# One fused kernel of linear attention and two feed-forward layers: the first chunk pipelined by a unit, loads and diagonals moved ahead, two kinds of state products issued together

## The chip, the cores and the metric

The kernel runs on one core of one Trainium2 chip. The metric is device time of one execution in microseconds (us); lower is better. The engines are called PE (matrix products), DVE (vector), ACT (activation), POOL and SP; SP issues the DMAs.

## What is computed

```python
def _attn_ref(r, k, v, w, u):            # B, H, S, D = 4, 8, 768, 48
    for t in range(S):
        cur = np.einsum('bhd,bhe->bhde', u[None] * kt, vt)
        y[:, :, t] = np.einsum('bhd,bhde->bhe', rt, state + cur)
        state = w[None, :, :, None] * state + np.einsum('bhd,bhe->bhde', kt, vt)

def _moe_ref(x, w_in, w_out):            # x: 3072 x 384, d_ff = 2048
    h = x @ w_in
    g = np.where(h > 0.0, h, np.exp(np.minimum(h, 0.0)) - 1.0)
    return g @ w_out

def _moe2_ref(x, w_in, w_out):
    h = x @ w_in
    return (h * np.cos(h)) @ w_out
```

The output is the second layer of the first layer of the attention, all in fp32. A recurrence over 768 steps with a decay per head and channel comes first; its output, as 3072 rows of 384, goes through both layers.

## The kernel before

The sequence is cut into six chunks of 128 steps (`NC`), and the heads into four pairs (`ORDER`, first 3, then 0, 1, 2). A chunk c and a pair j make a unit (c, j), 24 in all; each has the four batches of two heads. Inside a chunk the steps are split once more into an early and a late half of 64. A unit goes through these steps:

- `a_load`: its `trk` (r and k by channel) and `tnat` (r, k and v by time) are loaded. In the first chunk they are called `first_rk` and `first_nat` and lie in buffers of weights that come later.
- `a_scale` (DVE, line 210) multiplies `trk` by powers of the decay. `a_diag` (DVE, lines 224 to 227) forms the diagonal terms `a0`; ACT (line 233) then spreads them over a diagonal matrix `A`, eight instructions. `a_keys` (DVE, line 216 with the table `wn`) scales the keys.
- `gain(c, j, 1)` (PE, line 264) forms the early half's keys-by-values products, `gain(c, j, 0)` the late half's: the state sums. `a_scores` (PE, line 298) forms the scores.
- `a_mask` (DVE) copies the scores into `A` under a mask (line 306) and forms `mid`, the state at the middle of the chunk (line 311).
- `a_out` (PE): the products with `mid` and `st` (line 326), then `values` (line 277) for one half of the scores; `evict` (ACT, line 288) takes the output out of PSUM. `a_state` (DVE, line 337) forms the next state `st`.
- `a_next` does the other `values` of the unit before, the early `gain` and scores of the new one, the eviction and the mask. `a_pack` (SP, line 363) moves the finished output into the rows of `xraw`.

The first chunk runs by itself, unit after unit. While it runs, the first weight is fetched. Then a loop over `t` does the layers: sixteen `t` (tiles f of 128 hidden columns) make a block, one block per chunk and layer. In the first block of the first layer, the weights are unpacked and split as they come: `load_w`, `conv_abs` (ACT, line 86), `conv_low` (DVE, lines 92 and 95), `conv_high` (DVE, lines 102 and 108), `conv_split` (ACT line 131, DVE line 132). `ffn_in` (PE, line 396) makes nine products 128x512 per `t` in groups called wide here; `ffn_out_f32` and `ffn_out_t` (lines 447 and 454) follow two `t` later. `expn` (ACT) and `elu` (DVE, line 414) lie between.

Beside block b, the units of chunk b + 1 are done: `attn_items` sets at which `t` a step of a unit is issued. Each engine runs its instructions in the order in which the program issues them:

```python
            s0 = 4 * n - 3 if c > 1 else 2 + 3 * n
            items.append((s0 - 6, lambda j=j: a_load(c, j)))
            items.append((s0 - 2, lambda j=j: a_scale(c, j)))
            items.append((s0 - 1, lambda j=j: (a_diag(c, j), a_keys(c, j))))
            items.append((s0, lambda j=j, done=done: a_next(done, c, j)))
            items.append((s0 + 1, lambda j=j: (a_out(c, j), a_state(c, j))))
```

`count_safe` checks the decays (PE line 623) for a slower general path, which is not taken with these inputs.

Of the kernel before, what the change touches and what calls it, by code (L numbers as in the profile page):

```python
# [40 lines left out]
def fused_kernel(ctx: ExitStack, tc: tile.TileContext, rk, nat, wcol, urow, r, k, v, wu, w1, w2, out):  # L41
# [178 lines left out]
    def a_diag(c, j):  # L220
        u = units[c, j]
        tnat = u["nat"]
        q, key = (tnat[:, :, i].rearrange("p h e b d -> p h (e b d)") for i in range(2))
        nc.vector.tensor_tensor(out=q, in0=q, in1=key, op=ALU.mult)
        times(tnat[:, :, 0], ub, j)
        a0 = work.tile([P, 2 * B], F32, tag="a0", name="a0")
        nc.vector.tensor_reduce(  # L227
            out=a0.rearrange("p (h n) -> p h n", h=2), in_=tnat[:, :, 0].rearrange("p h e b d -> p h (e b) d"),
            axis=AX.X, op=ALU.add,
        )  # L230
        a = work.tile([P, 2 * B, SC], F32, tag="A", name="A")
        for n in range(2 * B):
            nc.scalar.activation(out=a[:, n], in_=eye, func=AF.Copy, scale=a0[:, n:n + 1])  # L233
        u["A"] = a

    def a_keys(c, j):
        times(units[c, j]["nat"][:, :, 1], wn, j)
# [17 lines left out]
    def gain(c, j, row):  # L255

        tnat = units[c, j]["nat"]
        keys = tnat.rearrange("p h x e b d -> p h (x e b d)")
        rs = slice(64 * row, 64 * row + 64)
# [22 lines left out]
    def evict(c, j, same):  # L282
        u = units[c, j]
        if same:
            u["yu"] = work.tile([RP, 2, 2, 2, SC], F32, tag="yu", name="yu")
        for e in range(2):
            row = e if same else 1 - e
            nc.scalar.activation(out=u["yu"][:, e, :, 1 - row], in_=outs(e)[0:RP, row], func=AF.Copy)

    def a_scores(c, j):  # L290
        trk = units[c, j]["rk"]
        gain(c, j, 1)
        for b in range(B):
            for row in range(2):
                for e in range(2):
                    ks, ts = late_early(row)
                    es = slice(64 * e, 64 * e + D)
                    nc.tensor.matmul(  # L298
                        banks[1 - e][ks, (B + b) * SC:(B + b + 1) * SC], trk[es, b // 2, 1, b % 2, ks],
                        trk[es, b // 2, 0, b % 2, ts], start=True, stop=True,  # L300
                    )
# [11 lines left out]
            op0=ALU.mult, op1=ALU.add,  # L313
        )

    def a_out(c, j):
# [13 lines left out]
        values(c, j, True)  # L330
        if c < NC - 1:
            gain(c, j, 0)
        evict(c, j, True)

    def a_state(c, j):
# [3 lines left out]
                in1=state_sums(0)[0:RP], op0=ALU.mult, op1=ALU.add,  # L339
            )  # L340

    def a_next(done, c, j):

        if done:
            values(*done, False)
        if c < NC:
            a_scores(c, j)
        if done:
            evict(*done, False)
        if c < NC:  # L350
            a_mask(c, j)

    def a_pack(c, j):

# [114 lines left out]
    def general():  # L469

        T, Q = 16, 4
        E = D // Q
        decay = work.tile([P, 2, D], F32, tag="yu", name="decay")
        nc.sync.dma_start(out=decay, in_=wu)
        s = work.tile([P, E, D], F32, tag="nat", name="s", bufs=3)
        nc.vector.memset(s, 0.0)
# [85 lines left out]
                    )  # L562


    def attn_items(c):

        items, packs = [], []
        for n, j in enumerate(ORDER):
            s0 = 4 * n - 3 if c > 1 else 2 + 3 * n
            s1 = 4 * n + 1 if c > 1 or n == HP - 1 else 5 + 3 * n  # L570
            done = (c, ORDER[n - 1]) if n else (c - 1, ORDER[-1]) if c > 1 else None
            items.append((s0 - 6, lambda j=j: a_load(c, j)))
            items.append((s0 - 2, lambda j=j: a_scale(c, j)))
            items.append((s0 - 1, lambda j=j: (a_diag(c, j), a_keys(c, j))))
            items.append((s0, lambda j=j, done=done: a_next(done, c, j)))
            items.append((s0 + 1, lambda j=j: (a_out(c, j), a_state(c, j))))
            if c == NC - 1 and n == HP - 1:
                items.append((s1, lambda j=j: a_next((c, j), NC, None)))
            packs.append((max(s1, 4), lambda j=j: a_pack(c, j)))
        items += packs  # L580
        return items

    def tables():
# [31 lines left out]
    def count_safe():  # L615

        ok = inv
        nc.vector.tensor_scalar(out=ok, in0=wc, scalar1=W_LOW, scalar2=None, op0=ALU.is_ge)
        nc.vector.scalar_tensor_tensor(
            out=ok, in0=wc, scalar=W_HIGH, in1=ok, op0=ALU.is_le, op1=ALU.mult  # L620
        )
        okp = psum.tile([1, HP], F32, tag="h", name="okp", bufs=2)
        nc.tensor.matmul(okp, ones[0:RP], ok, start=True, stop=True)
        nc.vector.tensor_reduce(out=count, in_=okp, axis=AX.X, op=ALU.add)
        nc.vector.tensor_scalar(
            out=safe, in0=count, scalar1=float(RP * HP), scalar2=None, op0=ALU.is_ge
        )

    with tc.manual_schedule():
# [32 lines left out]

        items = {}

        for c in range(NC - 1, 0, -1):
            for it, fn in attn_items(c):
                items.setdefault((c - 1) * NF + it, []).append(fn)
# [4 lines left out]
        table_rows()  # L672
        a_diag(0, ORDER[0])
        a_keys(0, ORDER[0])
        done = None
# [40 lines left out]
        for t in range(NT + 2):  # L716
# [3 lines left out]
            if layer == 0 or t == L:  # L720
                if t < NF - 1:
                    conv_split(t + 1)
                elif block == 1:
                    late_split(f)
                if t > 0:
                    gs[t - 1] = split_g(g) if t > NF else (g,)
                if f == NF - 1 and block + 1 < NC:
                    xs[block + 1] = [split_x(xin[block + 1], k) for k in range(KC)]
                if t == 2 * NF:
                    count_safe()  # L730
                if layer == 0:
# [118 lines left out]
```

## Time and profile before

| | |
|---|---|
| runs | 942.06, 937.43, 942.55 us; median 942.06 |
| profiled execution | 937.57 us, its span 935.9 us |
| PE busy | 893.5 us (95%) |
| DVE busy | 679.4 us (73%) |
| ACT busy | 495.5 us (53%) |
| DMA | 98.90 MB, mean 106 GB/s |
| mean granted clock of PE | 0.993 |

The span is what the trace covers, from the first to the last instruction. Busy shares are means over stages that differ: in the first, there is only the attention of one chunk; in the second, PE and DVE both work on the first block; later PE is busy nearly throughout.

### The profile page before, as it was taken

The page shows a single profiled execution, that of the slowest core. Times are in us where ns is not written, and L with a number is a line of the kernel's source. Part 1 is how long each engine was busy: PE and PEld are TensorE (multiplying, and loading weights), DVE is VectorE, ACT ScalarE, POOL GpSimd, SP SyncE. Part 2 cuts the span into 40 slices and gives each one's busy share as a digit, 9 for nine tenths or more (in the row PEclk, how much of TensorE's full clock was granted, in tenths as well). Part 3 has the DMA queues.
Part 4 walks back from the last instruction along what each step waited for, and adds up shares of the span by engine and source line. Part 5 has one row for each costly group of instructions (what it writes and reads, how often), then busy time and mean ns, then how long its engine had stood idle before and what let it go on. Part 6 is the DMA issues. An engine that isn't in the chain of part 4 may idle for free.

```text
span 935.9 us, 16782 instructions
## 1 busy us (share of the span) xinstructions
PE 893.5 (95%) x6730; PEld 746.4 (80%) x6730; DVE 679.4 (73%) x1164; ACT 495.5 (53%) x998; POOL 4.1 (0%) x18
## 2 busy tenths in 40 slices
PE   5459989999999999999999999999999999999996
PEld 5436556887878888788888899999999999999996
DVE  6579997878776776766534478778777777777775
ACT  2345556666755766656545545445444544444443
POOL 1000000000000000000000000000000000000000
PEclk9979999999999999999999999999999999999999
DMA  9177755444444543441165510200100200200001
GB/s 289 37 216 250 241 160 187 165 139 155 156 134 169 181 159 122 172 148 44 76 221 186 211 57 1 68 1 1 68 1 1 68 0 1 68 1 1 35 1 38
DMA packets 35687, 98.90 MB, mean 106 GB/s; under 512 B 4496, under 2 KB 14352, under 8 KB 35600
## 3 DMA queue, kind: packets, MB, share of 16 engines
q1 hardware_dynamic: 35600, 97.73, 31.3%
q8 instruction: 55, 0.90, 0.4%
q14 instruction: 32, 0.26, 0.1%
HBM read 67.83 MB, written 22.02 MB: 96 GB/s over the span
## 4 chain that ended last, share of the span: by engine, by line
PE 84%; DVE 8%; DMA 2%; ACT 1%; issue 1%; SPq 0%; DVEq 0%
PE ph L396 39%; PE acc L463 21%; PE acc L454 18%; DVE wx L108 1%; PE acc L447 1%; DVE wx L102 1%; PE yb L326 1%; PE yb L264 1%; PE yb L277 1%; PE yb L298 1%; DMA trk<-in_rk 1%; DVE trk L210 1%; DVE wx L95 1%; DVE wx L92 1%; DVE e L414 1%; DMA w<-wx 1%
## 5 line engine op out<-in xcount | busy, mean ns | idle before, releaser
L396 PE MATMUL ph<-xhl,w 128*128 128x512 f32 x1728 | 438.1, 398 | 14.6 <-DVE e L414 9.1
L396 PEld LDWEIGHTS ph<-xhl,w 128*128 128x128 f32 x1728 | 324.8, 189 | 89.0 <-ACT w L131 13.4
L463 PE MATMUL acc<-w,gh 128*128 128x384 f32 x768 | 195.4, 335 | 0.0
L454 PE MATMUL acc<-gh,w 128*128 128x512 f32 x480 | 165.7, 399 | 0.0
L463 PEld LDWEIGHTS acc<-w,gh 128*128 128x128 f32 x768 | 140.0, 188 | 7.9
L439 ACT ACTIVATE r<-r,pair 128x512 f32<-128x512 f32 x96 | 69.5, 724 | 126.7 <-DVE r L433 126.6
L463 PE MATMUL acc<-w,gl 128*128 128x384 f32 x384 | 129.0, 336 | 0.8 <-DVE gl L404 0.8
L427 DVE SCALAR_TENSOR_TENSOR r<-kk,ph 128x512 f32<-128x512 int32 x96 | 66.1, 688 | 62.7 <-ACT kk L422 61.9
L454 PEld LDWEIGHTS acc<-gh,w 128*128 128x128 f32 x480 | 90.1, 188 | 20.6
L414 DVE SCALAR_TENSOR_TENSOR e<-e,ph 128x512 f32<-128x512 f32 x96 | 65.5, 682 | 55.1 <-ACT e L410 55.0
L422 ACT ACTIVATE kk<-ph 128x512 int32<-128x512 f32 x96 | 57.4, 598 | 78.0 <-PE ph L396 78.0
L409 ACT ACTIVATE e<-ph 128x512 f32<-128x512 f32 x96 | 56.9, 593 | 71.3 <-PE ph L396 69.9
L454 PE MATMUL acc<-gl,w 128*128 128x512 f32 x240 | 94.1, 392 | 0.0
L403 ACT ACTIVATE gh<-e 128x512 fp32r<-128x512 f32 x80 | 50.2, 627 | 58.4 <-PE acc L454 54.2
L440 DVE TENSOR_TENSOR r<-r,ph 128x512 f32<-128x512 f32 x96 | 65.8, 686 | 20.9 <-ACT r L439 20.9
L404 DVE TENSOR_TENSOR gl<-e,gh 128x512 fp32r<-128x512 f32 x80 | 55.2, 690 | 33.4 <-ACT gh L403 33.3
L463 PEld LDWEIGHTS acc<-w,gl 128*128 128x128 f32 x384 | 72.1, 188 | 1.4 <-DVE gl L404 1.4
L430 DVE SCALAR_TENSOR_TENSOR r<-kk,r 128x512 f32<-128x512 int32 x96 | 66.4, 692 | 3.3
L404 DVE TENSOR_TENSOR gl<-r,gh 128x512 fp32r<-128x512 f32 x96 | 65.7, 685 | 0.8 <-ACT gh L403 0.8
L410 ACT ACTIVATE e<-e 128x512 f32<-128x512 f32 x96 | 60.6, 632 | 3.1
L233 ACT ACTIVATE A<-eye,a 128x64 f32<-128x64 f32 x192 | 48.5, 335 | 23.6 <-DVE a L227 23.6
L403 ACT ACTIVATE gh<-r 128x512 fp32r<-128x512 f32 x96 | 60.0, 625 | 1.1 <-DVE r L440 1.1
(90 smaller groups left out, 757.7 us busy)
## 6 DMA issues: line engine op xcount, KB each, us to landing
wraw<-in_w SPq DMA_DIRECT2D x32, 768.0 KB, 5.0
w2d<-wraw SPq DMA_DIRECT2D x16, 768.0 KB, 3.2
w<-w2d SPq DMA_DIRECT2D x16, 768.0 KB, 4.2
tnat<-in_nat SPq DMA_DIRECT2D x20, 576.0 KB, 7.4
trk<-in_rk SPq DMA_DIRECT2D x20, 448.0 KB, 5.9
x2d<-osb SPq DMA_DIRECT2D x6, 768.0 KB, 4.1
xraw<-x2d SPq DMA_DIRECT2D x6, 768.0 KB, 5.1
out_y<-yo SPq DMA_DIRECT2D x12, 384.0 KB, 3.0
```

The lines of the kernel that those rows point to most:

```text
L396: nc.tensor.matmul(ph, w[:, cs], z, start=(n == 0), stop=(n == 3 * KC - 1))
L403: nc.scalar.activation(out=gh, in_=g, func=AF.Copy)
L404: nc.vector.tensor_tensor(out=gl, in0=g, in1=gh.bitcast(F32), op=ALU.subtract)
L410: nc.scalar.activation(out=e, in_=e, func=AF.Exp, scale=-1.0)
L414: nc.vector.scalar_tensor_tensor(out=e, in0=e, scalar=-1.0, in1=ph, op0=ALU.add, op1=ALU.max)
L422: nc.scalar.activation(out=kk, in_=ph, func=AF.Copy, scale=1.0 / TWO_PI, bias=0.25)
L427: nc.vector.scalar_tensor_tensor(out=r, in0=kk, scalar=-C1, in1=ph, op0=ALU.mult, op1=ALU.add)
L430: nc.vector.scalar_tensor_tensor(out=r, in0=kk, scalar=-C2, in1=r, op0=ALU.mult, op1=ALU.add)
L439: nc.scalar.activation(out=r, in_=r, func=AF.Sin, bias=halfpi)
L440: nc.vector.tensor_tensor(out=r, in0=r, in1=ph, op=ALU.mult)
L454: nc.tensor.matmul(acc[m], w[:, cs], g, start=(f == 0 and n == 0), stop=(f == NF - 1 and n == 2))
L463: nc.tensor.matmul(acc[m][:, 0:DM], g[:, ts], w[:, DM:2 * DM], start=(f == 0 and n == 0), stop=(f == NF - 1 and n == 2),)
```

## The change

Five things change, and nothing of the arithmetic.

1. The diagonal work is split into `a_diag` (DVE) and `a_eye` (ACT). In the first chunk, diagonal, keys and `A` of a unit are issued ahead of the mask copy of the unit before. In the loop, diagonal and keys are issued in the slot of the unit before, and `a_load` two units ahead.
2. `gains(late, early)` takes the place of the two `gain` calls: the late products of a unit and the early ones of the next are issued in turn, and the late sums move to the bank `banks[0]`, behind the outputs.
3. The loads of the second chunk's first two units go out among the loads of the first weights.
4. `yu`, the evicted output, has three buffers instead of two.
5. `count_safe` keeps its DVE steps; the product and what follows are issued three `t` later, in `sum_safe`.

```diff
+    def gains(late, early):
         for b in range(B):
             for e in range(2):
-                m = D if e else 64
-                k0 = (4 + 2 * e + b % 2) * D
-                nc.tensor.matmul(
-                    state_sums(row)[64 * e:64 * e + m, b, :], keys[rs, b // 2, k0:k0 + m],
-                    tnat[rs, b // 2, 2, e, b % 2], start=True, stop=True,
-                )
+                for row, unit in enumerate((late, early)):
+                    if unit is None:
+                        continue
+                    tnat = units[unit]["nat"]
+                    keys = tnat.rearrange("p h x e b d -> p h (x e b d)")
+                    rs = slice(64 * row, 64 * row + 64)
+                    m = D if e else 64
+                    k0 = (4 + 2 * e + b % 2) * D
+                    nc.tensor.matmul(
+                        state_sums(row)[64 * e:64 * e + m, b, :], keys[rs, b // 2, k0:k0 + m],
+                        tnat[rs, b // 2, 2, e, b % 2], start=(row == 1), stop=True, skip_group_check=True,
+                    )
...
     def state_sums(row):
-        return banks[2][:, row * B * D:(row + 1) * B * D].rearrange("p (b d) -> p b d", b=B)
+        x = banks[2][:, 0:B * D] if row else banks[0][:, B * SC:B * (SC + D)]
+        return x.rearrange("p (b d) -> p b d", b=B)
...
-            u["yu"] = work.tile([RP, 2, 2, 2, SC], F32, tag="yu", name="yu")
+            u["yu"] = work.tile([RP, 2, 2, 2, SC], F32, tag="yu", name="yu", bufs=3)
...
-        for f in range(3):
-            load_w(0, f)
+        load_w(0, 0)
+        a_load(1, ORDER[0])
+        load_w(0, 1)
+        load_w(0, 2)
+        a_load(1, ORDER[1])
...
+        a_eye(0, ORDER[0])
+        gains(None, (0, ORDER[0]))
+        a_next(None, (0, ORDER[0]))
         for n, j in enumerate(ORDER):
-            a_next(done, 0, j)
-            a_out(0, j)
-            if done:
-                a_pack(*done)
-            done = (0, j)
+            new = (0, ORDER[n + 1]) if n + 1 < HP else (1, ORDER[0])
             if n + 1 < HP:
-                a_scale(0, ORDER[n + 1])
-                a_state(0, j)
-                a_diag(0, ORDER[n + 1])
-                a_keys(0, ORDER[n + 1])
+                a_diag(*new)
+                a_keys(*new)
+                a_eye(*new)
             else:
                 conv_abs(0, 0)
+                a_diag(*new)
+                a_keys(*new)
+            a_mask(0, j)
+            a_out(0, j, new)
+            if n + 1 < HP:
+                a_scale(*new)
+            else:
                 conv_low(0, 0)
-                a_state(0, j)
-        a_next(done, NC, None)
-        a_pack(*done)
+            a_state(0, j)
+            a_next((0, j), new if n + 1 < HP else None)
+            a_pack(0, j)
...
+            items.append((s0 + 1, lambda u=u, nxt=nxt: (a_out(*u, nxt), a_state(*u))))
+            items.append((s0 - 2, lambda u=u: a_scale(*u)))
+            items.append((s0 - 1, lambda u=u: a_eye(*u)))
+            if i > HP:
+                items.append((slot[last], lambda u=u: (a_diag(*u), a_keys(*u))))
+            if i >= HP + 2:
+                items.append((slot[every[i - 2]], lambda u=u: a_load(*u)))
```

Three places show the new order. On DVE in the first chunk, from the first unit's diagonal on; `first_nat` is r, k and v of a unit, `ub` and `wn` are tables. Before:

```order
L224 TENSOR_TENSOR first_nat<-first_nat 128x2x192
L216 TENSOR_TENSOR first_nat<-first_nat,ub 128x192 x2
L227 TENSOR_REDUCE a_195<-first_nat 128x8
L216 TENSOR_TENSOR first_nat<-first_nat,wn 128x192 x2
L306 COPY_PREDICATED A<-mask,yb 128x2x128 x2
L311 SCALAR_TENSOR_TENSOR mid<-yb,back,st 112x4x48
L210 TENSOR_TENSOR first_rk<-first_rk,pw 112x1024
L337 SCALAR_TENSOR_TENSOR st<-mid,pows,yb 112x4x48
```

With the change (the mask copy is line 313 now, `mid` 318, `st` 343):

```order
L227 TENSOR_REDUCE a_203<-first_nat 128x8
L216 TENSOR_TENSOR first_nat<-first_nat,wn 128x192 x2
L224 TENSOR_TENSOR first_nat<-first_nat 128x2x192
L216 TENSOR_TENSOR first_nat<-first_nat,ub 128x192 x2
L227 TENSOR_REDUCE a_243<-first_nat 128x8
L216 TENSOR_TENSOR first_nat<-first_nat,wn 128x192 x2
L313 COPY_PREDICATED A<-mask,yb 128x2x128 x2
L318 SCALAR_TENSOR_TENSOR mid<-yb,back,st 112x4x48
L210 TENSOR_TENSOR first_rk<-first_rk,pw 112x1024
L343 SCALAR_TENSOR_TENSOR st<-mid,pows,yb 112x4x48
```

The second unit's diagonal and keys now stand ahead of the first unit's mask copy.

On PE in a unit of the first chunk, from the `values` products on (line 285 now; state products 272, scores 305). Before, the late products, the other `values`, the early products of the next unit, and the scores:

```order
L277 MATMUL yb<-A,first_nat 48x64 x8
L264 MATMUL yb<-first_nat 64x48
L264 MATMUL yb<-first_nat 48x48
...
L277 MATMUL yb<-A,first_nat 48x64 x8
L264 MATMUL yb<-first_nat 64x48
L264 MATMUL yb<-first_nat 48x48
...
L298 MATMUL yb<-first_rk 64x64 x16
```

With the change:

```order
L285 MATMUL yb<-A,first_nat 48x64 x8
L272 MATMUL yb<-first_nat 64x48 x2
L272 MATMUL yb<-first_nat 48x48 x2
...
L285 MATMUL yb<-A,first_nat 48x64 x8
L305 MATMUL yb<-first_rk 64x64 x16
```

Each pair is one late product and one early product of the next unit; nothing stands between the other `values` and the scores any more.

On SP, the loads behind those of the first chunk (`wraw` is a packed weight). Before:

```order
L202 DMA first_nat<-in_nat 128x2x576
L77 DMA wraw<-in_w 128x1536 x3
L363 DMA xraw<-yu 32x256 x2
...
L130 DMA w_580<-wx 128x384
L77 DMA wraw<-in_w 128x1536 x2
L199 DMA trk<-in_rk 112x2x512
L202 DMA tnat<-in_nat 128x2x576
```

With the change:

```order
L202 DMA first_nat<-in_nat 128x2x576
L77 DMA wraw<-in_w 128x1536
L199 DMA trk<-in_rk 112x2x512
L202 DMA tnat<-in_nat 128x2x576
L77 DMA wraw<-in_w 128x1536 x2
L199 DMA trk<-in_rk 112x2x512
L202 DMA tnat<-in_nat 128x2x576
L367 DMA xraw<-yu 32x256 x2
```

Both units' loads stand ahead of the first packs; before, they stood behind two more weights.

## Rows read from the trace of the kernel before

**Rows 1.** The page's slices of PE; busy us of PE, PEld, DVE, ACT, POOL.

```profile
PE   5459989999999999999999999999999999999996
...
62.88:142.55 79.67, 76.52 (x814) 48.47 (x815) 75.21 (x132) 43.85 (x107) 0.00 (x0) 0.96 0.65 206
```

**Rows 2.** Timeline of the first chunk, 21 to 30: start us, us, engine, line.

```profile
21.11 0.77 DVE L306 COPY_PREDICATED A<-mask,yb 128x256 f32<-128x256 uint32 x2 [2.33 <-ACT yu L288]
22.34 0.71 PE L326 MATMUL yb<-first_rk,mid 48*64 48x64 f32 x16 [1.80 <-DVE mid L311]
...
23.21 0.68 PE L277 MATMUL yb<-A,first_nat 64*48 64x64 f32 x16
23.64 0.86 PE L264 MATMUL yb<-first_nat 64*64 64x48 f32 x14
23.91 0.45 ACT L288 ACTIVATE yu<-yb 112x128 f32<-112x128 f32 x2 [2.84 <-PE yb L277]
...
24.73 0.41 DVE L337 SCALAR_TENSOR_TENSOR st<-mid,pows,yb 112x192 f32<-112x192 f32 x1 [1.40 <-PE yb L264]
25.06 0.55 DVE L224 TENSOR_TENSOR first_nat<-first_nat 128x384 f32<-128x384 f32 x1
...
26.77 0.62 DVE L216 TENSOR_TENSOR first_nat<-first_nat,wn 128x192 f32<-128x192 f32 x2
...
27.18 0.77 PE L264 MATMUL yb<-first_nat 64*64 64x48 f32 x11 [2.08 <-DVE first_nat L216]
...
29.24 0.45 ACT L288 ACTIVATE yu<-yb 112x128 f32<-112x128 f32 x2 [0.27 <-PE yb L298]
```

**Rows 3.** Mask copies of units 1 and 4; second unit's `first_nat`: issue, landing.

```profile
12.56 0.77 DVE L306 COPY_PREDICATED A<-mask,yb 128x256 f32<-128x256 uint32 x2 [1.91 <-PE yb L298]
...
38.33 0.77 DVE L306 COPY_PREDICATED A<-mask,yb 128x256 f32<-128x256 uint32 x2 [2.33 <-ACT yu L288]
...
3.23 0.47 SPq L202 DMA_DIRECT2D first_nat<-in_nat  x1
...
DMA to landing us min/median/max: 9.2/9.2/9.2
```

**Rows 4.** Timeline 44 to 64, and the window 60 to 62 (clock third from the end).

```profile
44.85 0.96 DVE L108 SCALAR_TENSOR_TENSOR wx<-wraw,wx 128x768 int32<-128x768 int32 x1
...
52.13 0.43 SPq L199 DMA_DIRECT2D trk<-in_rk  x1
...
58.60 1.23 DVE L210 TENSOR_TENSOR trk<-trk,pw 112x1024 f32<-112x1024 f32 x1 [5.76 <-DMA trk<-in_rk]
...
61.92 0.96 DVE L108 SCALAR_TENSOR_TENSOR wx<-wraw,wx 128x768 int32<-128x768 int32 x1
...
63.62 4.24 PE L396 MATMUL ph<-xhl,w 128*128 128x512 f32 x9 [8.62 <-DVE e L414]
...
60.00:62.00 2.00, 0.00 (x0) 0.00 (x0) 1.90 (x4) 0.00 (x0) 0.00 (x0) 0.50 1.05 284
```

**Rows 5.** Timeline of PE in a later unit: start us, us, tile, passes.

```profile
300.21 0.46 PE L326 MATMUL yb<-trk,mid 48*64 48x64 f32 x16
...
300.70 0.43 PE L277 MATMUL yb<-A,tnat 64*48 64x64 f32 x16
300.93 0.63 PE L264 MATMUL yb<-tnat 64*48 64x48 f32 x16
301.49 0.51 PE L454 MATMUL acc<-gh,w 128*128 128x512 f32 x1
...
314.34 0.44 PE L264 MATMUL yb<-tnat 64*64 64x48 f32 x10
...
315.37 0.51 PE L454 MATMUL acc<-gh,w 128*128 128x512 f32 x1
```

**Rows 6.** Waits of PE after 60 us, of SP to 146; the page's loads.

```profile
PE okp L623 <- DVE inv L619: 0.8, 1, 0.8
...
SPq L202 <- PE yb L277: 2.2, 1, 2.2
...
tnat<-in_nat SPq DMA_DIRECT2D x20, 576.0 KB, 7.4
```

More of the change, by code (lines that the diff above doesn't have):

```diff
@@ L230, in a_diag, with a_eye @@
         )
-        a = work.tile([P, 2 * B, SC], F32, tag="A", name="A")
+        u["a0"] = a0
+    def a_eye(c, j):
+        u = units[c, j]
+        a0 = u.pop("a0")
+        u["A"] = a = work.tile([P, 2 * B, SC], F32, tag="A", name="A")
         for n in range(2 * B):
             nc.scalar.activation(out=a[:, n], in_=eye, func=AF.Copy, scale=a0[:, n:n + 1])
-        u["A"] = a
     def a_keys(c, j):
@@ L252, in state_sums @@
     def state_sums(row):
-        return banks[2][:, row * B * D:(row + 1) * B * D].rearrange("p (b d) -> p b d", b=B)
[L255 to L259, printed above, removed]
+        x = banks[2][:, 0:B * D] if row else banks[0][:, B * SC:B * (SC + D)]
+        return x.rearrange("p (b d) -> p b d", b=B)
+    def gains(late, early):
         for b in range(B):
             for e in range(2):
-                m = D if e else 64
-                k0 = (4 + 2 * e + b % 2) * D
-                nc.tensor.matmul(
-                    state_sums(row)[64 * e:64 * e + m, b, :], keys[rs, b // 2, k0:k0 + m],
-                    tnat[rs, b // 2, 2, e, b % 2], start=True, stop=True,
-                )
+                for row, unit in enumerate((late, early)):
[10 more added lines that the diff above has]
+                    )
     def values(c, j, same):
@@ L291, in a_scores @@
         trk = units[c, j]["rk"]
-        gain(c, j, 1)
         for b in range(B):
@@ L314, in a_mask, with a_out @@
         )
-    def a_out(c, j):
+    def a_out(c, j, after):
         trk = units[c, j]["rk"]
@@ L330, in a_out @@
         values(c, j, True)
-        if c < NC - 1:
-            gain(c, j, 0)
+        gains((c, j) if c < NC - 1 else None, after)
         evict(c, j, True)
@@ L340, in a_state, with a_next @@
             )
-    def a_next(done, c, j):
+    def a_next(done, new):
         if done:
             values(*done, False)
-        if c < NC:
-            a_scores(c, j)
+        if new:
+            a_scores(*new)
         if done:
             evict(*done, False)
-        if c < NC:
-            a_mask(c, j)
     def a_pack(c, j):
@@ L472, in general @@
         E = D // Q
-        decay = work.tile([P, 2, D], F32, tag="yu", name="decay")
+        decay = work.tile([P, 2, D], F32, tag="yu", name="decay", bufs=3)
         nc.sync.dma_start(out=decay, in_=wu)
@@ L562, in general, with attn_items @@
                     )
[L565 to L580, printed above, removed]
+    def attn_items():
+        every = [(c, j) for c in range(NC) for j in ORDER]
+        slot = {(0, ORDER[-1]): -2}
+        for u in every[HP:]:
+            n = ORDER.index(u[1])
+            slot[u] = 2 + 3 * n if u[0] == 1 else NF * (u[0] - 1) + 4 * n - 3
+        slot[None] = slot[every[-1]] + 4
+        items = []
+        for i in range(HP, len(every) + 1):
+            last, u = every[i - 1], every[i] if i < len(every) else None
+            s0 = slot[u]
+            nxt = every[i + 1] if i + 1 < len(every) else None
+            items.append((s0, lambda last=last, u=u: a_next(last if last[0] else None, u)))
+            if last[0]:
+                at = s0 if last[1] != ORDER[0] or last[0] == 1 else s0 + 3
+                items.append((at, lambda last=last: a_pack(*last)))
+            if u is None:
+                continue
+            items.append((s0, lambda u=u: a_mask(*u)))
+            items.append((s0 + 1, lambda u=u, nxt=nxt: (a_out(*u, nxt), a_state(*u))))
[5 more added lines that the diff above has]
+                items.append((slot[every[i - 2]], lambda u=u: a_load(*u)))
         return items
@@ L621, in count_safe, with sum_safe @@
         )
+    def sum_safe():
+        ok = inv
         okp = psum.tile([1, HP], F32, tag="h", name="okp", bufs=2)
@@ L663, in fused_kernel @@
         items = {}
-        for c in range(NC - 1, 0, -1):
-            for it, fn in attn_items(c):
-                items.setdefault((c - 1) * NF + it, []).append(fn)
+        for it, fn in attn_items():
+            items.setdefault(it, []).append(fn)
         banks.append(psum.tile([P, 512], F32, tag="ys", name="yb"))
@@ L674, in fused_kernel @@
         a_keys(0, ORDER[0])
-        done = None
+        a_eye(0, ORDER[0])
+        gains(None, (0, ORDER[0]))
+        a_next(None, (0, ORDER[0]))
         for n, j in enumerate(ORDER):
-            a_next(done, 0, j)
-            a_out(0, j)
-            if done:
-                a_pack(*done)
-            done = (0, j)
+            new = (0, ORDER[n + 1]) if n + 1 < HP else (1, ORDER[0])
             if n + 1 < HP:
-                a_scale(0, ORDER[n + 1])
-                a_state(0, j)
-                a_diag(0, ORDER[n + 1])
-                a_keys(0, ORDER[n + 1])
+                a_diag(*new)
+                a_keys(*new)
+                a_eye(*new)
             else:
                 conv_abs(0, 0)
+                a_diag(*new)
[5 more added lines that the diff above has]
+            else:
                 conv_low(0, 0)
-                a_state(0, j)
-        a_next(done, NC, None)
-        a_pack(*done)
+            a_state(0, j)
+            a_next((0, j), new if n + 1 < HP else None)
+            a_pack(0, j)
         conv_high(0, 0)
@@ L730, in fused_kernel @@
                     count_safe()
+                if t == 2 * NF + 3:
+                    sum_safe()
                 if layer == 0:
```

## The prediction

> **What bounds the kernel now.** I read the slices of the page first, then windows, then the timeline where PE idles. Each slice is 23.4 us: PE is under 90% in the first three, the sixth and the last [rows 1]. From the seventh on it is full, so that only less PE work saves time there; earlier, whatever it waits for does. Between 62.88 and 142.55 us, while the first weights are converted, DVE is busy 75.21 of 79.67 us and PE 76.52 [rows 1]. Both are nearly full, and DVE's conversions set when each next weight is ready. So a microsecond taken out ahead of the third weight tile (f = 2) comes off the end only as far as DVE is also earlier.
>
> In the first chunk one unit takes 8.6 us (mask copy at 12.56, at 38.33 for the fourth [rows 2, 3]). One long chain fills it: mask copy, `mid`, PE's products, `st`, then the diagonal and key scaling of the next unit on DVE, then its early state products and scores on PE, then eviction, then the next mask copy. After it comes the gap that PE feels most: DVE stands still for 5.76 us until `trk` of the second chunk's first unit lands, 6.5 us after its issue at 52.13 [rows 4].
>
> **First chunk, four units.** The change puts diagonal and keys of unit n+1 ahead of the mask copy of unit n, and the early state products of n+1 behind the late ones of n. The first mask copy now stands behind the second unit's diagonal, which needs its `first_nat`: issued at 3.23, landed 9.2 later, at 12.4 [rows 3]. The diagonal and keys take 2.33 us (25.06 to 26.77 + 0.62 [rows 2]), so the first mask copy moves from 12.56 to 14.8: 2.2 us lost.
>
> The new period, from one mask copy on, by [rows 2]: to PE's first product 1.23 (21.11 to 22.34); 48 passes to the state products 1.30 (to 23.64); 32 state passes at 37 ns, the pace of the 48 passes of early products and scores (27.18 to 28.97, that is 0.27 before the eviction at 29.24), 1.19; from the last pass to the eviction 0.27 (23.64 to 23.91), of which half, 0.22, must be over since the late sums now share a bank with what it reads. At 4.2 `st` starts, 0.41. Then the other value products, 0.43 (23.21 to 23.64), scores 32 x 37 ns = 1.18, tail 0.27, eviction 0.45, and some 0.2 for hand-overs: 7.15 in all. DVE's own way (`st`, then 2.33 of diagonal and keys) ends at 7.0, just inside. So the fourth mask copy stands at 14.8 + 3 x 7.15 = 36.2, not 38.33: **2.1 us won**. Bounds: at 8.6 it would come 2.3 late; with passes paced as in [rows 5] the period is 5.1 and it comes 8.2 early. I take 7.15, since the same passes stand in this very stretch.
>
> **To the third weight.** Before, the first weight's conversion ends at 44.85 + 0.96 = 45.81 [rows 4], 7.48 after the fourth mask copy. Now `st` starts 4.2 after it, and two conversions of 0.96 follow: 6.6, **0.9 won**. From there to the third weight's conversion (end 62.88) it was 17.07, of which 5.76 was the wait for `trk`. That load now goes out right behind the first weight's, in the first 15 us: **5.8 won**. What is late next is DVE itself. PE's gap before f = 2 shrinks from 8.62 us to about 2.8. It stood at the lower level, a granted clock of 0.50, at 60 to 62 [rows 4]; whether it falls now costs nothing in the sum, as DVE is later than PE by then.
>
> The loads pay for this: 1.0 MB stands ahead of the second and third weight and as much behind them, on one queue. The rows give a landing of 9.2 us for such a load in a full queue; the second weight is not read before the fourth mask copy, at 36, so the first chunk covers it. The packs of the first unit queue behind all this, and their buffers are three instead of two; if that cover failed, the fourth unit's eviction would wait.
>
> **While DVE is full.** The diagonal and keys of (1, 3) leave this stretch for the first chunk, where they lie beside PE's chain: **2.3 won**. The other units' diagonals move by one slot and stay. Eviction, `st` and the other values wait on more than before, but the scores are three slots away; behind the eviction ACT's next weight copy waits 0.2 to 0.4 us, as it did for other reasons. Nothing counted.
>
> **State products later.** In a unit of the later chunks the late products take 0.56 us for 16 passes (300.93 to 301.49), early ones and scores together 1.03 for 48 (314.34 to 315.37) [rows 5]: 1.59 for 64 passes. In both, neighbours among state products read the same half of the partitions. Now they alternate halves, in the order of the scores. At 21.5 ns (1.03 / 48) all 64 cost 1.38: 0.21 won a unit. Chunks 2 to 4 have 12 such units under a full PE: **2.5 won**; those of chunk 1 hide under DVE. Bounds: at 15.3 ns (the 32 out products, 300.21 to 300.70) 7.3; if the paired 32 keep the late products' 35 ns, 2.6 lost. I take 21.5, as it is the nearest in order and holds the switch to the wide products.
> The Trainium skill (TensorE: Matmul & The Clock Gate, "Back-to-back issue gap") says that passes of up to 64 columns never start closer than about 25 ns. The out products here stand 15.3 ns apart, so the trace disagrees. By the page 64 passes would cost 1.6 us, an estimate, and this term would be nil.
>
> **The count of safe decays** is split: its product comes three slots after its DVE steps. PE waited 0.8 us for them [rows 6]: **0.8 won**.
>
> **Sum:** 2.1 + 0.9 + 5.8 + 2.3 + 2.5 + 0.8 = 14.4 us. The profiled execution took 937.57 (span 935.9, with 1.7 around it), so such a run comes to 923.2. The runs shown are 937.43, 942.06 and 942.55: the median is 4.5 above the profiled one, and nothing in the trace tells why. I subtract from the mean of the four, 939.9: **925.5 us**.
>
> **Rivals.**
> *State products stay apart.* They take 35 ns each even when paired. For: the late products do now. Against: the out products at 15.3 ns lie on alternating halves. The term turns from +2.5 to -2.6: 930.6. By the 25 ns of the Trainium skill's page above it would be a milder case of the same, 928.0.
> *The first chunk's period does not shrink.* The new chain through eviction, `st`, other values and scores takes as long as the old one. For: it has the same passes, and bank by bank waits. Against: 2.33 us of DVE work leave it. It costs 4.4: 929.9.
> *PE runs fast in the first chunk.* With PE less broken up, passes go as in [rows 5]. For: DVE is then the only bound, and 5.1 a unit. Against: although the granted clock reads 1.00 in this stretch, the passes are 1.8 times as far apart as later. The fourth mask copy comes 6.1 earlier still: 919.4.
> *Loads reach DVE late: slower.* A unit's load is now issued two units ahead, behind the other values of the unit before on PE, and its diagonal comes three slots later, not five. In the full stretch a late `tnat` stops DVE and all conversions behind it. Such loads land in 7.4 us at the median [rows 6], the one wait of this kind for PE was 2.2, and three slots are some 17 us: 7 to spare. It decides from 17 us on; slower needs over 19 us in all, five for each of four units: 945.
> That the change doesn't do what it says I rule out from the order of the instructions.
>
> **How the numbers follow.** Forecast 0.64, state products apart 0.12, no shorter period 0.10, fast first chunk 0.09, late loads 0.05. A measurement of this kernel can tell about 0.5%, 4.7 us. All but the last are faster by more, though a mix of two misses comes near: faster 0.91, same 0.05, slower 0.04. The range goes from 915 (fast first chunk, less the spread of runs) to 933 (a period that stays and products apart, with some pay elsewhere).
>
> **What would show it.** Right: mask copies some 7.1 us apart from 14.8 on; no wait of DVE for `trk`; PE's third group of wide products near 54.5 instead of 63.62, the next ones each some 10 us earlier than before; state products and scores at about 1.4 us a unit; no wait for the count. Wrong: a DVE wait for `tnat`, a period over 8, PE idle after 150 us, or a lead at 150 us that is not kept to the end.

## The result, and the profile after

The changed kernel takes 928.74 us (median of four runs, 927.53 to 929.33), the kernel before 939.74 in runs beside them: a ratio of 0.988, 95% interval 0.984 to 0.992. It is faster, by 11.0 us, and 3.2 above the forecast of 925.5. The profiled execution took 927.53, its span 925.8; the span of before was 935.9, so the traces differ by 10.1.

The busy times and PE's slices on the page of the changed kernel, against the busy times of before and [rows 1] (lines now: wide 400, `values` 285, state products 272, out products 333, eviction 296, mask copy 313, `st` 343, `elu` 418):

```profile
PE 890.8 (96%) x6730; PEld 739.9 (80%) x6730; DVE 678.7 (73%) x1164; ACT 491.8 (53%) x998; POOL 4.0 (0%) x18
...
PE   5598989999999999999999999999999999999996
```

The third slice fills up. The fourth falls from 9 to 8: something is given back there.

The timeline of the changed kernel, to be held against [rows 2 to 4]:

```profile
13.54 0.77 DVE L313 COPY_PREDICATED A<-mask,yb 128x256 f32<-128x256 uint32 x2
...
15.99 1.07 PE L272 MATMUL yb<-first_nat 64*48 64x48 f32 x32
17.11 0.44 ACT L296 ACTIVATE yu<-yb 112x128 f32<-112x128 f32 x2 [1.97 <-PE yb L272]
17.43 0.41 DVE L343 SCALAR_TENSOR_TENSOR st<-mid,pows,yb 112x192 f32<-112x192 f32 x1 [1.68 <-ACT yu L296]
...
20.02 0.77 DVE L313 COPY_PREDICATED A<-mask,yb 128x256 f32<-128x256 uint32 x2
...
33.15 0.77 DVE L313 COPY_PREDICATED A<-mask,yb 128x256 f32<-128x256 uint32 x2
...
38.49 0.96 DVE L108 SCALAR_TENSOR_TENSOR wx<-wraw,wx 128x768 int32<-128x768 int32 x1
...
46.92 1.22 DVE L210 TENSOR_TENSOR trk<-trk,pw 112x1024 f32<-112x1024 f32 x1
50.23 0.96 DVE L108 SCALAR_TENSOR_TENSOR wx<-wraw,wx 128x768 int32<-128x768 int32 x1
51.93 2.58 PE L400 MATMUL ph<-xhl,w 128*128 128x512 f32 x9 [1.09 <-DVE e L418]
...
134.61 0.96 DVE L108 SCALAR_TENSOR_TENSOR wx<-wraw,wx 128x768 int32<-128x768 int32 x1
...
136.31 0.96 PE L400 MATMUL ph<-xhl,w 128*128 128x512 f32 x2 [0.54 <-DVE e L418]
...
515.29 2.25 PE L400 MATMUL ph<-xhl,w 128*128 128x512 f32 x9
```

Two wide groups of before are needed beside those rows, that of the sixteenth tile and one at the end of the first layer; they answer to the last two rows above:

```profile
144.48 0.80 PE L396 MATMUL ph<-xhl,w 128*128 128x512 f32 x1
...
529.74 2.22 PE L396 MATMUL ph<-xhl,w 128*128 128x512 f32 x9
```

The mask copies stand 6.5 us apart, not 8.6. The scaling of `trk` waits for nothing (46.92). How far the changed kernel is ahead, by the same instruction in both traces:

| place | before | after | ahead | forecast |
|---|---|---|---|---|
| fourth mask copy | 38.33 | 33.15 | 5.2 | 2.1 |
| third weight converted | 62.88 | 51.19 | 11.7 | 8.8 |
| sixteenth weight converted | 142.55 | 135.57 | 7.0 | 11.1 |
| sixteenth tile's wide group | 144.48 | 136.31 | 8.2 | 11.1 |
| end of the first layer | 529.74 | 515.29 | 14.5 | 14.4 |
| end of the span | 935.9 | 925.8 | 10.1 | 14.4 |

So the sum was right at the end of the first layer, where 14.5 stood against 14.4, by terms that missed in both directions; and 4.4 were lost again in the second layer, whose code the change does not touch. The experiments ask three things: what gave back 4.7 while DVE was full, what gave back 4.4 in the second layer, and whether the terms that held did so for the reason named.

### The profile page after: what moved, and what is told of

Its sections match the earlier page's. It is cut to its first block, busy times and chain, and to the rows that moved or that the text cites. A ratio compares the mean times of both kernels' runs of the same rounds, so it can differ in the third digit from the quotient of the medians.

```text
span 925.8 us, 16771 instructions
## 1 busy us (share of the span) xinstructions
PE 890.8 (96%) x6730; PEld 739.9 (80%) x6730; DVE 678.7 (73%) x1164; ACT 491.8 (53%) x998; POOL 4.0 (0%) x18
## 4 chain that ended last, share of the span: by engine, by line
PE 85%; DVE 8%; ACT 4%; DMA 1%; issue 1%; SPq 0%; ACTq 0%; DVEq 0%
PE ph L400 40%; PE acc L467 22%; PE acc L458 19%; PE yb L333 1%; PE yb L285 1%; DVE wx L108 1%; DVE wx L102 1%; PE yb L272 1%; DMA first_nat<-in_nat 1%; ACT A L238 1%; PE yb L305 1%; PE acc L451 1%; ACT w L131 1%; ACT e L413 1%; DVE A L313 1%
## 5 line engine op out<-in xcount | busy, mean ns | idle before, releaser
L407 ACT ACTIVATE gh<-e 128x512 fp32r<-128x512 f32 x80 | 50.2, 628 | 76.6 <-DVE e L418 49.3
L458 PEld LDWEIGHTS acc<-gl,w 128*128 128x128 f32 x240 | 45.1, 188 | 8.2
```

The costliest lines, as they stand in the source:

```text
L407: nc.scalar.activation(out=gh, in_=g, func=AF.Copy)
L458: nc.tensor.matmul(acc[m], w[:, cs], g, start=(f == 0 and n == 0), stop=(f == NF - 1 and n == 2))
```

## The second layer: addresses or pace

The order in which buffers are first taken changed with the loads, and `yu` grew; so the wide products' inputs lie elsewhere in SBUF. Three kernels move addresses alone, or nearly.

**lay_before:** all buffers where the kernel before had them, `yu` with two.

```diff
...
         nc.sync.dma_start(out=wc, in_=wcol)
+        work.tile([P, 2 * DM, 2], I32, tag="wraw", name="wraw", bufs=3)
+        work.tile([P, 2 * B, SC], F32, tag="A", name="A")
+        work.tile([P, 2 * B], F32, tag="a0", name="a0")
+        work.tile([RP, 2, 2, 2, SC], F32, tag="yu", name="yu", bufs=2)
+        work.tile([P, KC, TB], F32, tag="xraw", name="xraw", bufs=1)
+        work.tile([P, 2 * DM], I32, tag="wx", name="wx", bufs=3)
+        for n in range(KC):
+            work.tile([P, 2, TB], F32R, tag=f"x{n}", name="xhl", bufs=1)
```

> The changed kernel with its buffers in SBUF put back exactly where the kernel before had them: the tags are taken once in the old order at the start, and `yu` has two buffers again. No instruction on any engine moves. Layout theory: in the second layer, whose code the change does not touch, the lead over the kernel before fell from 14.46 to 10.0 us, with output products 176 ns apart instead of 173.9; the addresses alone did that, so two wide groups there take 8.29 us again instead of 8.35 to 8.43, and the time falls by 4.4, to about 924.3. Rival: the chip was a little slower in that execution and the addresses do nothing; time 928.7, and the second layer's pace differs from run to run whatever the layout.

**lay_before_yu3:** the same lines, `yu` with three buffers.

> As the one above, but with three buffers of `yu`, so that everything allocated behind them lies 2,048 bytes higher than in the kernel before. Layout theory: if the inputs of the wide products (xhl) in relation to rk and nat matter, time as above, 924.3; if the 2,048 bytes of gh and gl matter, 928.7. Theory that the third `yu` buffer is what the first chunk needs: same first chunk as in the changed kernel here, and mask copies later than at 20.0, 26.6 and 33.2 us in the one above. Rival on the layout: 928.7 for both.

**before_new_layout:** the kernel before, with `wraw`, `rk` and `nat` taken first and three buffers of `yu`.

> The kernel before with the changed kernel's addresses: rk and nat taken first, three buffers of `yu`; no instruction moves. Layout theory: 4.4 us slower in the second layer, 944.1 against 939.7. Rival, addresses do nothing: 939.7, same.

Measured: 931.12, 927.47 and 942.37 us (before beside them 940.57). Then the kernel before by itself once more:

**before_again**

> The kernel before once more, unchanged, for a second trace. Its runs so far lie in two groups, 936.7 to 939.0 and 940.6 to 942.3. Theory: what parts them is the pace of the second layer, and the profiled execution (937.57, output products 173.9 ns apart) was of the first group; an execution of the second group shows 176 to 177 ns there and about 3.5 us more in that layer. Rival: the groups differ in the first chunk, by the clock there, and the second layer always goes at 173.9 ns.

It took 940.56. Two wide groups of the second layer, the second of them 87 groups behind the first, on the timelines of before, of before_again and of the changed kernel:

```profile
533.86 2.22 PE L396 MATMUL ph<-xhl,w 128*128 128x512 f32 x9
...
894.62 2.23 PE L396 MATMUL ph<-xhl,w 128*128 128x512 f32 x9
```

```profile
532.99 2.22 PE L396 MATMUL ph<-xhl,w 128*128 128x512 f32 x9
...
897.22 2.23 PE L396 MATMUL ph<-xhl,w 128*128 128x512 f32 x9
```

```profile
519.44 0.86 PE L400 MATMUL ph<-xhl,w 128*128 128x512 f32 x3
...
884.19 1.10 PE L400 MATMUL ph<-xhl,w 128*128 128x512 f32 x4
```

That is 360.76, 364.23 and 364.75 us for the same work. One kernel with the same addresses shows two paces 3.47 apart; output products start 174 ns apart in the one and 177 in the other. **Shown:** 3.5 of the 4.0 us in these rows also lie between two executions of the kernel before, so that neither the change nor the layout is needed for them; lay_before, with the old addresses to the byte, went at 364.23 too. Whether the changed kernel can go at the faster pace at all is another question, taken up below. The other 0.5 is the new addresses: all seven traces of kernels that have them, before_new_layout among them, show 364.75. Twelve groups take 50.56 us there in every other block and 50.1 in the blocks between, and 50.2 in every block of before_again. The time of before_new_layout came to 1.0032 of before (1.0015 to 1.0048): neither theory's number, but more than nothing.

The runs fit this. The 51 later runs of before lie in two groups, 23 from 936.5 to 939.1 and 28 from 940.4 to 944.3, and none between. Ratios here are against this mixture. What chooses the pace was not found.

**after_again**

> The changed kernel once more, unchanged, to hold its time against the kernel before on one chip in more runs, and to see whether it ever shows the faster pace in the second layer that about half of the executions of the kernel before show. Theory: its addresses of the inputs in every other block shut that pace out; all runs between 927.5 and 930, two wide groups in 8.35 and 8.43 us. Rival: the pace falls by chance; then some runs near 924.5.

928.29 us, all six runs between 927.33 and 930.58, before beside them 940.73; ratio 0.9878, 0.9856 to 0.9899. None is near 924.5. Whether the new addresses shut the faster pace out stays open. For it: none of the twelve runs of before_new_layout came below 940.87, where 23 of 51 of before did, and none of the seven traces is faster than 364.75. Against it: the old addresses do not bring the faster pace back to the changed code. The traces of lay_before, lay_before_yu3, and of all_three and two_and_addresses further down all show 364.23, and the six runs of lay_before_yu3 (926.68 to 928.36) lie together too. Only early_loads below, the kernel before with another order of loads, showed 360.76 again. So the change may have cost the faster pace in some other way, or the draws were unlucky.

The third `yu` buffer has its own effect. In lay_before the eviction of the third unit waits for a pack:

```profile
26.09 0.77 DVE L313 COPY_PREDICATED A<-mask,yb 128x256 f32<-128x256 uint32 x2
...
32.76 0.44 ACT L296 ACTIVATE yu<-yb 112x128 f32<-112x128 f32 x2 [4.82 <-DMA xraw<-yu]
...
35.66 0.77 DVE L313 COPY_PREDICATED A<-mask,yb 128x256 f32<-128x256 uint32 x2
```

The last period is 9.6 us instead of 6.6; in the program's order the packs now stand behind the second chunk's loads. Three buffers are worth 3.0 us there, 3.7 in the time (931.12 to 927.47). They belong to early loads and a short period together: early_loads below has two buffers and the long period, and its fourth mask copy, at 37.97, is not late.

## The stretch in which DVE is full

**early_loads:** the kernel before with the early loads alone, at the old addresses.

```diff
...
-        for f in range(3):
-            load_w(0, f)
+        load_w(0, 0)
+        a_load(1, ORDER[0])
+        load_w(0, 1)
+        load_w(0, 2)
+        a_load(1, ORDER[1])
...
-            items.append((s0 - 6, lambda j=j: a_load(c, j)))
+            if c > 1 or n > 1:
+                items.append((s0 - 6, lambda j=j: a_load(c, j)))
```

> The kernel before with one part of the change alone: the loads of the second chunk's first two units go out among those of the first weights, buffers at the addresses that they had. The 5.76 us wait of DVE for `trk` goes, so the third wide group starts at about 57.9 instead of 63.62. Theory of the prediction, that what is won ahead of the DVE-full stretch is kept through it: 5.8 at the end, 934.8 against 940.6. Rival, that this stretch gives back part of any lead (in the changed kernel 14.3 us became 8.2): the lead falls to some 3.4 by the sixteenth tile, 937.2.

933.12 us against 938.98, ratio 0.9939 (0.9915 to 0.9962). Its trace:

```profile
57.41 2.96 PE L396 MATMUL ph<-xhl,w 128*128 128x512 f32 x6 [2.08 <-DVE e L414]
...
128.51 0.54 PE L277 MATMUL yb<-A,tnat 64*48 64x64 f32 x13 [1.81 <-ACT yu L288]
...
135.40 0.96 DVE L108 SCALAR_TENSOR_TENSOR wx<-wraw,wx 128x768 int32<-128x768 int32 x1
```

```profile
130.00:132.00 2.00, 2.00 (x19) 1.16 (x12) 1.31 (x3) 1.78 (x5) 0.00 (x0) 0.50 0.26 98
```

The third wide group starts 6.2 earlier, and the sixteenth conversion still ends 6.2 earlier (136.36 against 142.55). So the stretch by itself gives nothing of DVE's lead back: the rival falls. PE was 4.6 ahead by then and stayed so. After its wait of 1.81 us at 128.5, which before has too, the granted clock stood at 0.50 from 130 to 132 (the lower level); before, it read 1.00 there. That goes with the last 1.6 lost; no run separates the two.

**diag_slot**

```diff
-                items.append((slot[last], lambda u=u: (a_diag(*u), a_keys(*u))))
+                items.append((slot[last] - 1, lambda u=u: (a_diag(*u), a_keys(*u))))
```

> The changed kernel with diagonal and keys of a unit one slot earlier, in the slot before the one with the mask copy of the unit ahead, which had the least DVE work. Theory of uneven slots: the 2.3 us of diagonal and keys in the slot of the mask copy (0.77 twice, and mid) make the `elu` of that slot late, PE waits for `elu` 7.0 us in all in eight places; evened out, up to 4 of it goes: 924.7. Rival one: in a stretch where DVE is full only the sum of its work counts: 928.7. Rival two: loads now have two slots, some 11.5 us, until they are read, 7.4 at the median to land; if one comes late DVE and all behind it stands: over 930.

929.71 us, 1 above the changed kernel. Waits between 51 and 143:

```profile
PE ph L400 <- DVE e L418: 7.9, 8, 2.1
DVE st L343 <- ACT yu L296: 3.8, 5, 0.8
DVE A L313 <- ACT yu L296: 3.7, 4, 0.9
...
DVE tnat L224 <- DMA tnat<-in_nat: 0.5, 1, 0.5
```

My theory of uneven slots falls: PE's waits for `elu` are 7.9 us as against 7.0, and from the third to the sixteenth conversion (ends 51.75 and 136.43) it takes 84.7 us as against 84.4. Rival one holds, with one short wait for a load.

**st_first:** `st` between the two evictions of its slot.

```diff
...
-        evict(c, j, True)
+        if c == 0:
+            evict(c, j, True)
+        else:
+            evict(c, j, True, (1,))
+            a_state(c, j)
+            evict(c, j, True, (0,))
...
```

> The changed kernel; after the first chunk the eviction of the bank without the state sums is issued first, then `st`, then the eviction of the bank with the late sums, so that `st` no longer waits for an eviction; DVE's order is unchanged. Theory: the four waits of `st` in the DVE-full stretch, 3.02 us together, are DVE time that nothing covers; they go, the lead at the sixteenth tile rises from 8.2 to about 11, 925.7. Rival: DVE waits at the next conversion instead for a weight copy of ACT, which now stands behind `st`: 928.7.

925.20 us, ratio 0.9848 (0.9823 to 0.9873). **mask_between**, on top of it:

```diff
...
         for e in range(2):
+            if done and e == 0:
+                evict(*done, False, (0,))
             nc.vector.copy_predicated(
...
+        if done:
+            evict(*done, False, (1,))
         nc.vector.scalar_tensor_tensor(
             out=mid[:, j % 2, :, 0:D], in0=state_sums(1)[0:RP], scalar=back[:, j:j + 1], in1=st[:, j, :, 0:D],
...
```

> The kernel of st_first with one more step: in the loop the two mask copies of a unit and the two evictions of the unit before are issued in turn (eviction of bank 0, mask copy from bank 1, mask copy from bank 0, eviction of bank 1), so that the first mask copy waits for no eviction. Theory, as for `st`: the four waits of the mask copy in the DVE-full stretch, 3.7 us together, are DVE time that nothing covers, and most of it goes: 922, the lead at the sixteenth tile 14 instead of 11.1. Rival: PE is the bound by then and the scores arrive no earlier; 925.2 as in st_first.

923.25 us, ratio 0.9828 (0.9806 to 0.985). Waits between 51 and 140 in the changed kernel, in st_first, in mask_between, and before (51 to 149):

```profile
PE ph L400 <- DVE e L418: 7.0, 8, 1.4
DVE st L343 <- ACT yu L296: 3.8, 5, 0.8
DVE A L313 <- ACT yu L296: 3.7, 4, 0.9
```

```profile
PE ph L405 <- DVE e L423: 5.5, 7, 2.8
DVE A L313 <- ACT yu L296: 3.7, 4, 0.9
```

```profile
PE ph L409 <- DVE e L427: 4.6, 5, 2.8
...
DVE A L315 <- ACT yu L296: 1.6, 4, 0.4
```

```profile
DVE A L306 <- ACT yu L288: 2.8, 3, 0.9
```

And the windows from the end of the third to the end of the sixteenth conversion, of the same three (us, then busy us of PE, PEld, DVE); of before it is the row in [rows 1]:

```profile
51.19:135.57 84.38, 76.94 (x819) 45.61 (x819) 75.66 (x132) 42.72 (x107) 0.00 (x0) 1.00 0.66 202
```

```profile
51.31:132.70 81.39, 77.79 (x819) 46.83 (x819) 75.43 (x132) 42.83 (x107) 0.00 (x0) 0.98 0.67 209
```

```profile
50.83:130.12 79.29, 76.80 (x819) 46.53 (x819) 75.53 (x132) 42.80 (x107) 0.00 (x0) 0.98 0.68 214
```

This is the answer. DVE executes 132 instructions in the stretch in every kernel, 75.2 to 75.7 us; what differs is its idle time: 4.5 before, 8.7 after, 6.0 without the waits of `st`, 3.8 without most of those of the mask copy. **Shown:** of 4.7 us given back, 4.3 are new idle time of DVE. The wait of `st` for the eviction, which the change brought by putting the late sums into the bank that the eviction reads, is the most of it. Four of the five waits in the rows, 3.0 us, lie in the stretch (the fifth is at 137.5); without them the stretch is 3.0 shorter and the time 3.1 to 3.5 (925.20 against 928.29 and 928.74). The waits of the mask copy, 2.8 us before and 3.7 now, make 0.9 more. PE's waits for `elu` shrink along with it: 7.0, 5.5, 4.6.

The Trainium skill (PSUM — Partial Sum Buffer, "PSUM bank collisions raise a hardware error") says that two engines may not touch one bank in the same partitions at once, two readers included. The waits agree: 0.8 us at most for a `st` and an eviction that read different columns of one bank. What happens without the wait no run here shows.

## State products, and the best version

**unpaired**

```diff
-        for b in range(B):
-            for e in range(2):
-                for row, unit in enumerate((late, early)):
-                    if unit is None:
-                        continue
+        for row, unit in enumerate((late, early)):
+            if unit is None:
+                continue
+            for b in range(B):
+                for e in range(2):
```

> The changed kernel with the late products of a unit issued first and the early ones of the next unit behind them, instead of in turn; same place, same banks. Theory that the alternation of halves is what pays: the 32 passes go from 18 back to some 35 ns for the late ones and 32 for the early ones, 0.46 us per unit, times 12 units under a full PE is 5.5 us: 934.2. Rival: the pairing does nothing and the 0.46 us per unit came from the products standing together in one place instead of two: 928.7.

930.83 us, 2.1 to 2.5 above the changed kernel. The unit near 300 us on PE's timeline, the changed kernel, then unpaired:

```profile
307.19 0.43 PE L285 MATMUL yb<-A,tnat 64*48 64x64 f32 x16
307.42 0.66 PE L272 MATMUL yb<-tnat 64*48 64x48 f32 x32
```

```profile
291.82 0.91 PE L272 MATMUL yb<-tnat 64*48 64x48 f32 x32
```

Taking turns is worth 0.25 us a unit for the 32 state passes, 3.0 over twelve units. From start to start in the units between 230 and 380 us, the 32 state passes of a unit take 900 ns before (28.1 each), 842 unpaired (26.3) and 588 paired (18.4); a score pass takes 21.4 ns before and 18.0 in both others, where no early product stands among the scores any more. So both theories hold in part.

**all_three** and **two_and_addresses** look for the best version. The first adds to mask_between the same turn of mask copies and evictions in the first chunk, half of the diagonal ahead of `st` there, and the old addresses with three `yu`; the second only the addresses. The core of the first chunk's edit:

```diff
+            a_diag(*new, 1 if n else 2)
+            a_keys(*new)
+            a_mask(*u, done)
...
+                a_scale(*new)
+                a_diag(*firsts[n + 2], 0)
...
+            a_state(*u)
```

> The kernel of mask_between, with the same turn of mask copies and evictions in the first chunk, where product and `ub` step of the next diagonal also go ahead of `st` into the 1.7 us in which DVE waits for PE, and with the addresses of the kernel before (three buffers of `yu`). Theory: the first chunk's period is the chain over PE, ACT and DVE, 6.57 us; diagonal work of 1.2 us leaves the part behind `st` and the mask copy no longer waits for it nor for the eviction: some 6.15, three periods, 1.3 us won; 1.2 more in the second layer from the addresses: 2.5 below mask_between. Rival: the period stays at 6.57, and only the addresses show.

> The kernel of mask_between with the addresses of the kernel before and three buffers of `yu`; no instruction moves. It stands between mask_between (923.25) and all_three (921.71), and tells what in all_three came from the addresses and what from the first chunk. Theory: the addresses give 1.2, so 922.0, and the first chunk's part gives next to nothing. Rival: the first chunk's part gave all of it: 923.2.

921.71 (ratio 0.9819, 0.9793 to 0.9844) and 921.75 us (0.981, 0.9788 to 0.9833). The addresses give the 1.5 below mask_between (0.5 of it in the 87 groups of the second layer: 364.23 against 364.75), the first chunk's edit nothing that can be told. The mask copies of all_three do come sooner, but one waits for an eviction, and the inputs of the first tile for a pack:

```profile
26.00 0.77 DVE L318 COPY_PREDICATED A<-mask,yb 128x256 f32<-128x256 uint32 x2 [1.15 <-ACT yu L299]
...
32.12 0.77 DVE L318 COPY_PREDICATED A<-mask,yb 128x256 f32<-128x256 uint32 x2 [0.73 <-PE yb L308]
...
39.98 0.63 ACT L400 ACTIVATE xhl<-xraw 128x512 fp32r<-128x512 f32 x1 [0.53 <-DMA xraw<-yu]
```

Three periods take 18.7 us there and 19.6 in two_and_addresses; by the fourth wide group all_three is 2.0 behind all the same (58.95 against 56.91). The granted clock read 0.66 from 52 to 58 us there and 1.00 in the other, so what the edit gives at one clock stays open. The simpler two_and_addresses is the version to keep, 6.5 below the changed kernel beside it (928.29).

## Why the prediction was right, and where its steps failed

The sign and the size were right: the forecast's mechanism, five gains ahead of and under the first block's DVE work, is what the traces show. Step by step:

- *First chunk, 2.1 won:* mis-sized, 5.2. The first mask copy stood at 13.54, not 14.8: `first_nat` had landed 1 us sooner. The period was 6.5, not 7.15: I priced state passes and scores at 37 ns, and the 32 paired passes with their tail took 1.12 (15.99 to 17.11) instead of 1.46. The 37 ns was a mean over two kinds: in the stretch of [rows 2] the first early products start 46 ns apart and the later scores 31; with the change, state passes in turn and scores both start 25 ns apart. Out of turn the state passes need 39 ns, and yet the period of unpaired is the same (mask copies at 20.60, 27.11 and 33.63), since its eviction waits only for the late half of them. It starts at 17.70, while the passes run to 18.13:

```profile
16.61 1.52 PE L272 MATMUL yb<-first_nat 64*48 64x48 f32 x32
17.70 0.45 ACT L296 ACTIVATE yu<-yb 112x128 f32<-112x128 f32 x2 [1.94 <-PE yb L272]
```

  The rival of an unchanged period falls; that of a PE at its later pace (5.1) does not hold either, the measured period lies between.
- *To the first conversion, 0.9:* 1.2. *The wait for `trk`, 5.8:* from the first to the third conversion 5.3 were won here and 5.9 by itself in early_loads; right. The cover that I named for the packs, a third buffer, was needed: without it 3.7 are lost.
- *While DVE is full, 2.3 won and nothing counted for waits:* **this step failed**, and in two ways. The diagonal of (1, 3) does leave the stretch, but that of (2, 0), the second unit of the next chunk, comes in at its end, right behind the mask copy of (2, 3) (second row below). I wrote that the other diagonals move by one slot and stay; this one moves by three, from `t` = 16 to 13. So DVE has 132 instructions in the stretch before and after; this part was counted, not tried by itself. And the waits of `st`: I saw that it would wait on more, asked only whether PE's scores come late by it, and costed it at nothing. They came to 3.0 us in the stretch, on the engine that bounds it; one is the first row. I had looked at who waits behind the eviction on ACT, and not at what DVE loses. 4.7 lost instead of 2.3 won.

```profile
123.66 0.41 DVE L343 SCALAR_TENSOR_TENSOR st<-mid,pows,yb 112x192 f32<-112x192 f32 x1 [0.76 <-ACT yu L296]
...
130.19 0.55 DVE L224 TENSOR_TENSOR tnat<-tnat 128x384 f32<-128x384 f32 x1
```

- *State products, 2.5:* 3.0 by the pairing alone; by the same rows 0.7 more for the state products that now stand in one place (900 to 842 ns a unit) and 1.3 by the scores (32 passes, 3.4 ns), over twelve units. The Trainium skill's rule (TensorE: Matmul & The Clock Gate, "Back-to-back issue gap"), no passes closer than about 25 ns, would have made this nil; state passes at 18.4 and scores at 18.0 ns speak against it once more.
- *Count product, 0.8:* there is no wait for it left; not tried apart. From the sixteenth tile to the end of the first layer 6.3 us are won, of which state products, scores and this wait make 5.8; the rest is not traced.
- *The base:* I subtracted from the mean of the runs because nothing told why they differed. The second layer's pace does: the profiled execution of before had the faster one, and that is 3.5 of the 4.4 by which its trace gains there.
- *Late loads:* no wait of DVE for `tnat` in the changed kernel's stretch, and 0.5 with a slot less. The rival falls.

That the errors cancelled was chance: +2.9 by the third weight, -7.0 up to the sixteenth, then +4.2, of which PE's passes make 2.5 (5.0 won instead of 2.5). Experiments on one part of a change at a time showed it; the end time could not.

## What to carry to other kernels

When partial results move to another PSUM bank, list every reader of that bank on every engine. Here two readers of different columns waited for each other, and on the engine that bounds the stretch the waits were paid in full: 3.0 us of waits, 3.0 us of the stretch. Issuing first the eviction that shares no bank and next the reader on the bounding engine took them away. A step moved ahead in a pipeline leaves a stretch only if the next one does not move into it: count the instructions of the bounding engine between the same two points. And before a difference is explained, look at where in the two traces it arises; if the code there is the same, profile the old kernel twice.

## What the runs showed of the hardware that was not expected

- The second layer of one unchanged kernel has two paces: 360.76 and 364.23 us for the same 87 groups, with output products 174 or 177 ns apart and the granted clock at 1.00 in both. A third, 364.75, is that of all seven traces at the new addresses.
- The first chunk does not feel the granted clock. In after_again it stood at 0.50 from 13 to 34 us:

```profile
13.00:34.00 21.00, 11.74 (x384) 10.76 (x384) 15.55 (x37) 8.23 (x36) 0.00 (x0) 0.50 0.95 289
```

```profile
14.68 0.77 DVE L313 COPY_PREDICATED A<-mask,yb 128x256 f32<-128x256 uint32 x2
...
34.28 0.77 DVE L313 COPY_PREDICATED A<-mask,yb 128x256 f32<-128x256 uint32 x2
```

  Three periods take 19.60 us there, and 19.61 in the changed kernel's first trace, at 1.00. The price came with the wide products: the first group started 1.14 later than in that trace, as the mask copies had, the third 2.67 (54.60 against 51.93) and the fourth 4.19, and 3.05 were left at the end (930.58 against 927.53). It is not a fixed price: another run of after_again, at a mean granted clock of 0.976 against 0.998 in that first trace, took 927.33.
